# Warm-up matmuls between the first steps, exps spread over blocks, eight plain blocks first, three banks for eight blocks: one change to a linear-attention-and-MLP kernel

## The chip, the cores and the metric

The kernel runs on one core of one Trainium2 chip. The metric is the device time of one execution in microseconds (us). A profile of the same execution shows a span that is about 1.8 us shorter than that time. Each timed run also records the mean clock that TensorE was granted. For a comparison, the changed kernel and the kernel before ran in turn on the same chip; "ratio" below is the mean time of one kernel's fast runs over the mean of the other's in the same rounds, so it is not quite the ratio of the medians that are quoted.

## The reference, cut to what matters

```
# q, k, v: (8 batches, 8 heads, 576 positions, 64), float32
q_s = exp(q - max_d q);  q_s = q_s / sum_d q_s
k_s = exp(k - max_s k);  k_s = k_s / sum_s k_s
kv  = einsum('bhsd,bhse->bhde', k_s, v)
x   = einsum('bhsd,bhde->bhse', q_s, kv)       # then (4608, 512)
h   = x @ w_in                                  # (512, 2048)
g   = h * sigmoid(h)
out = g @ w_out                                 # (2048, 512)
```

## The kernel before

The work is cut into nine chunks of 512 rows; a batch has 576 rows. For chunk 0 the first product is done over the whole of batch 0 in 16 "wide" blocks of 576 columns. For the others it is done in 16 blocks `mm1` of 512 columns. After each block ScalarE computes a tanh into `sg` and VectorE multiplies it into `GT` (this is the silu), which frees the block's bank of the accumulator `PS`. The second product is plain for chunk 0 (16 blocks `mm2_plain`) and a seven-product scheme (`prod`) from chunk 1 on. That scheme needs differences of the weights (`t_op`: T1 to T4, once) and of the activations (`s_op`: S1 to S4, per chunk), all on VectorE. Between the blocks, a list of plans places the attention steps of the next batch: exps on ScalarE, sums on GpSimd or VectorE, normalisation of q, a transposition of q (by TensorE for batches 0 and 1, by a transposing DMA from batch 2 on), a key-value product on TensorE, and the input product `xt` of the next chunk.

The program hands each engine its instructions in the order in which they are written; a plan at unit `u` is written before block `u`.

```
def mm1(t, fb):
    bank = hb[0] % (2 if t == 1 else 3)        # chunk 1 has two banks, later chunks three
    hb[0] += 1
    mm1_mm(t, fb, bank, range(NC))
    mm1_silu(t, fb, bank)                      # ScalarE tanh, then VectorE product
...
def mm2_plain(t, fc):                          # uses banks 2 to 5
    for tb in range(4):
        nc.tensor.matmul(out=PS[:, 2 + tb, :], lhsT=GTS[t % 2][:, fc, ...], rhs=W2[:, fc, :], ...)
...
def heat(n, bank=5):                           # warm-up: the result is never read
    for _ in range(n):
        nc.tensor.matmul(out=PS[:, bank, :], lhsT=warm[:, 0:128], rhs=warm, start=True, stop=True)
...
heat(20)
... loads issued by GpSimd in this order: W1 (five parts), batch 1's q and k,
    W2[0:4], batch 1's v, W2[4:8]
...
# chunk 0's plain blocks and chunk 1's blocks a1 (b1 is the first of these units)
units += [lambda i=i: mm2_plain(0, i) for i in range(6)] + a1[:1]
for i in range(6, NFB):
    units += [a1[i - 5], lambda i=i: mm2_plain(0, i)]
units += a1[NFB - 5:]
...
plan(b1, lambda: (tr(1, 0, 0, 5, 6), tr(1, 0, 5, J, 7)))        # first transposition, batch 1
plan(b1 + 2, lambda: (tr(1, 1, 0, 5, 6), tr(1, 1, 5, J, 7)))    # second transposition
plan(b1 + 3, lambda: kv_both(1))
...
plan(b1 + 18, lambda: q_transpose(2))                           # the transposing DMA, batch 2
plan(b1 + 23, lambda: kv_both(2))
plan(b1 + 28, lambda: t_op(3, nc.vector, 0, 4))                 # T3
plan(b1 + 30, lambda: t_op(3, nc.vector, 4, 8))
for i, x in enumerate((28, 30)):
    plan(b1 + x, lambda i=i: xt(2, i))                          # needs the transposed q of batch 2
plan(begin[2], lambda: (mm2_plain_out(0), hb.__setitem__(0, 0)))  # evictions of banks 2 to 5
```

The softmax here doesn't subtract the row's maximum and nothing guards it: scores larger than these inputs give would overflow.

Of the kernel before, what the change touches and what calls it, by code (L numbers as in the profile page):

```python
# [17 lines left out]
def kernel(  # L18
# [72 lines left out]
    def load(b, name, src, cc, eng):  # L91
        t = ld.tile([128, 2, J * D], FP32, name=name)
        st[b][name, cc] = t
        x = src[b].rearrange("(g r) (p j) d -> g (r p) (j d)", r=2, j=J)
        eng.dma_start(out=t, in_=x.rearrange("g x y -> x g y")[:, 2 * cc:2 * cc + 2, :])  # L95
# [7 lines left out]
    def exp_q(b, cc):  # L103
        if "eq" not in st[b]:
            st[b]["eq"] = ap.tile([128, J, NG * D], BF16, name="eq", bufs=2)
        nc.scalar.activation(out=half(st[b]["eq"], cc), in_=jgd(b, "qt", cc), func=ACT.Exp)  # L106

    def exp_k(b, cc):
        nc.scalar.activation(out=half(ek, cc), in_=jgd(b, "kt", cc), func=ACT.Exp)  # L109

    def vcast(b, cc, eng, g0=0, g1=2):
        o = vaug[:, :, 2 * cc + g0:2 * cc + g1, 0:D]
        i = jgd(b, "vt", cc)[:, :, g0:g1, :]
        copy(eng, o, i)

    def qsum_pair(b, cc):
        e = half(st[b]["eq"], cc)
        t1 = ap.tile([128, J, 2, D // 2], FP32, name="t1")
        t2 = ap.tile([128, J, 2, D // 4], FP32, name="t2", bufs=2)
        nc.gpsimd.tensor_tensor(  # L120
            out=t1, in0=e[:, :, :, 0:D // 2], in1=e[:, :, :, D // 2:D], op=ALU.add
        )
        nc.gpsimd.tensor_tensor(
            out=t2, in0=t1[:, :, :, 0:D // 4], in1=t1[:, :, :, D // 4:D // 2], op=ALU.add
        )
        st[b]["t2", cc] = t2

    def qsum_end(b, cc):
        new_zq(b)
        nc.vector.reduce_sum(out=st[b]["zq"][:, cc], in_=st[b]["t2", cc], axis=AX.X)  # L130
        nc.vector.reciprocal(out=st[b]["rzq"][:, cc], in_=st[b]["zq"][:, cc])
# [16 lines left out]
    def qnorm(b, cc, eng):  # L148
        e = half(st[b]["eq"], cc)
        r = st[b]["rzq"][:, cc]  # L150
        eng.tensor_tensor(  # L151
            out=e, in0=e, in1=r[:, :, :, None].to_broadcast([128, J, 2, D]), op=ALU.mult
        )
# [12 lines left out]
    def tr(b, cc, j0, j1, bank):  # L166
        t = PS[:, bank, :].bitcast(BF16)
        for j in range(j0, j1):
            nc.tensor.transpose(  # L169
                out=t[:, (j - j0) * 128:(j - j0 + 1) * 128],  # L170
                in_=st[b]["eq"][:, j, cc * 128:(cc + 1) * 128],
                identity=ident,
            )

    def trcopy(b, cc, j0, j1, bank, eng=nc.vector):
        t = PS[:, bank, :].bitcast(BF16)[:, 0:(j1 - j0) * 128].rearrange("x (j y) -> x j y", y=128)
        copy(eng, new_qt(b)[:, j0:j1, cc, :], t)
# [13 lines left out]
    def kvcopy(b, c0=0, c1=2):  # L191
        kp = PS[:, 6:8, 0:256].rearrange("p r (c x) -> p r c x", x=128)[:, :, c0:c1, 0:E1]
        rz = ap.tile([128, 2, 2], FP32, name="rz", bufs=2)[:, :, 0:c1 - c0]
        nc.vector.reciprocal(out=rz, in_=kp[:, :, :, D])
        for c in range(c0, c1):
            nc.vector.tensor_tensor(
                out=kvn[b % 3][:, c],
                in0=kp[:, :, c - c0, 0:D],
                in1=rz[:, :, c - c0, None].to_broadcast([128, 2, D]),
                op=ALU.mult,  # L200
            )

    def kv_both(b):
        kv(b, 0)
        kv(b, 1)
        kvcopy(b)
# [11 lines left out]
    def xt_mm(b, cc, col, n, bank, dst):  # L218
        for r in range(2):
            for s in range(2):  # L220
                h = slice(s * 64, (s + 1) * 64)
                nc.tensor.matmul(  # L222
                    out=PS[r * 64:(r + 1) * 64, bank + s, dst:dst + n],
                    lhsT=kvn[b % 3][h, cc, r, :],
                    rhs=st[b]["qT"][h, col // P:(col + n) // P, cc, r * 64:(r + 1) * 64],
                )

    def xt_evac(t, cc, bank, d0, d1, o0, eng):
        o = XTS[t % 2][:, 2 * cc:2 * cc + 2, o0:o0 + d1 - d0]
        copy(eng, o, PS[:, bank:bank + 2, d0:d1])  # L230
# [33 lines left out]
            GTS[0][:, fb, :].rearrange("p (a n) -> p a n", a=2), S,  # L264
        )

    hb = [0]

    def mm1_mm(t, fb, bank, cs):
        o0 = pieces(t)[0][3]  # L270
# [11 lines left out]
        silu(t, fb, PS[:, bank, o0:TCH], GTS[t % 2][:, fb, o0:TCH], TCH - o0)  # L282

    def mm1(t, fb):
        bank = hb[0] % (2 if t == 1 else 3)
        hb[0] += 1
        mm1_mm(t, fb, bank, range(NC))
        mm1_silu(t, fb, bank)
# [10 lines left out]
    def mm2_plain(t, fc):  # L299
        for tb in range(4):  # L300
            nc.tensor.matmul(  # L301
                out=PS[:, 2 + tb, :],
                lhsT=GTS[t % 2][:, fc, tb * 128:(tb + 1) * 128],
                rhs=W2[:, fc, :],
                start=(fc == 0),
                stop=(fc == NFB - 1),
            )

    def mm2_plain_out(t):
        for ms in ((1, 2), (3, 0)):  # L310
            ow = mp.tile([128, 2, DM], FP32, name="ow", bufs=3)
            for i, m in enumerate(ms):
                if i == 0:
                    nc.scalar.activation(out=ow[:, i], in_=PS[:, 2 + m], func=ACT.Copy, scale=OS)
                else:
                    nc.vector.tensor_scalar_mul(out=ow[:, i], in0=PS[:, 2 + m], scalar1=OS)
                store(t, m * 128, ow[:, i])
# [116 lines left out]
    def heat(n, bank=5):  # L434
        for _ in range(n):
            nc.tensor.matmul(out=PS[:, bank, :], lhsT=warm[:, 0:128], rhs=warm, start=True, stop=True)
# [7 lines left out]
    def load_w2(f0, f1):  # L444
        nc.gpsimd.dma_start(
            out=W2[:, f0:f1, :],
            in_=w_out[f0 * 128:f1 * 128, :].rearrange("(fc p) o -> p fc o", p=128),
        )
# [34 lines left out]
    exp_k(0, 1)  # L483
    xt_mm(0, 0, 0, 320, 4, 0)
    xt_mm(0, 0, 320, 256, 0, 0)
    vcast(0, 1, nc.scalar, 0, 1)
    vcast(0, 1, nc.vector, 1, 2)
    trcopy(0, 1, 0, 5, 2, nc.scalar)
    trcopy(0, 1, 5, J, 3)
    kv(0, 1)  # L490
    kvcopy(0, 1, 2)
    xt_evac(0, 0, 4, 0, 320, 0, nc.scalar)
    xt_evac(0, 0, 0, 0, 256, 320, nc.vector)
    xt_mm(0, 1, 0, 320, 6, 0)
# [10 lines left out]
    def plan(u, f):  # L505
        at.setdefault(u, []).append(f)
# [26 lines left out]
    ORDER = (1, 5, 6, 2, 7, 4, 3)  # L533
    a1 = a_units(1)

    units += [lambda i=i: mm2_plain(0, i) for i in range(6)] + a1[:1]
    for i in range(6, NFB):
        units += [a1[i - 5], lambda i=i: mm2_plain(0, i)]
    units += a1[NFB - 5:]
    for t in range(2, NCH):  # L540
        begin[t] = len(units)
        bs = b_units(t - 1, ORDER)
# [76 lines left out]
            for cc in range(2):  # L619
                load(b, name, src, cc, eng)  # L620

    plan(8, lambda: (exp_q(1, 0), qsum_pair(1, 0)))
    plan(9, lambda: exp_q(1, 1))
    plan(11, lambda: (qsum_end(1, 0), qnorm(1, 0, nc.gpsimd), qsum_pair(1, 1)))
    plan(12, lambda: exp_k(1, 0))
    plan(13, lambda: load_w2(8, 12))
    plan(14, lambda: exp_k(1, 1))
    plan(b1, lambda: (tr(1, 0, 0, 5, 6), tr(1, 0, 5, J, 7)))
    plan(b1, lambda: (qsum_end(1, 1), qnorm(1, 1, nc.vector)))
    plan(b1, lambda: (trcopy(1, 0, 0, 5, 6, nc.scalar), trcopy(1, 0, 5, J, 7)))  # L630
    plan(b1, lambda: (vcast(1, 0, nc.scalar, 0, 1), vcast(1, 0, nc.vector, 1, 2)))
    plan(b1, lambda: (load_w2(12, 16), load(2, "qt", q, 0, nc.gpsimd)))
    plan(b1, lambda: nc.gpsimd.tensor_copy(GTS[1][:, :, 0:64], GTS[0][:, :, TCH:S]))
    plan(b1, lambda: (load(2, "qt", q, 1, nc.gpsimd), load(2, "kt", k, 0, nc.gpsimd)))
    plan(b1 + 2, lambda: (tr(1, 1, 0, 5, 6), tr(1, 1, 5, J, 7)))
    plan(b1 + 2, lambda: (trcopy(1, 1, 0, 5, 6, nc.scalar), trcopy(1, 1, 5, J, 7)))
    plan(b1 + 2, lambda: (vcast(1, 1, nc.scalar, 0, 1), vcast(1, 1, nc.vector, 1, 2)))
    plan(b1 + 2, lambda: load(2, "kt", k, 1, nc.gpsimd))
    plan(b1 + 3, lambda: kv_both(1))
    plan(b1 + 4, lambda: (load(2, "vt", v, 0, nc.gpsimd), load(2, "vt", v, 1, nc.gpsimd)))  # L640
    plan(b1 + 4, lambda: xt(1, 0))
    plan(b1 + 5, lambda: xt(1, 1))

    plan(b1 + 9, lambda: t_op(1, nc.vector, 0, 4))
    plan(b1 + 11, lambda: t_op(1, nc.vector, 4, 8))
    for i, x in enumerate((12, 14)):
        plan(b1 + x, lambda i=i: exp_q(2, i))
        plan(b1 + x + 1, lambda i=i: qsum(2, i, 0))
# [2 lines left out]
    plan(b1 + 18, lambda: q_transpose(2))  # L651
    for i, x in enumerate((19, 21)):
        plan(b1 + x, lambda i=i: vcast(2, i, nc.scalar))
    plan(b1 + 23, lambda: t_op(2, nc.vector, 0, 4))
    plan(b1 + 24, lambda: t_op(2, nc.vector, 4, 8))
    plan(b1 + 25, lambda: t_op(4, nc.vector, 0, 4))
    plan(b1 + 26, lambda: t_op(4, nc.vector, 4, 8))
    plan(b1 + 28, lambda: t_op(3, nc.vector, 0, 4))
    plan(b1 + 30, lambda: t_op(3, nc.vector, 4, 8))
    plan(b1 + 23, lambda: kv_both(2))  # L660
    plan(b1 + 22, lambda: loads(3, nc.sync))
    for i, x in enumerate((28, 30)):
        plan(b1 + x, lambda i=i: xt(2, i))
    plan(begin[2], lambda: (mm2_plain_out(0), hb.__setitem__(0, 0)))

    for t in range(2, NCH - 1):
        b = t + 1
# [58 lines left out]
```

## Time and profile before

| | before |
|---|---|
| time, median of 3 runs | 277.97 us (277.51 to 278.47) |
| span of the profiled execution | 276.2 us |
| TensorE busy | 262.9 us (95%) |
| mean granted clock in that execution | 0.991 |
| first `prod` of chunk 1's output (the start of chunk 2's stretch) | 69.40 us |

The first fence is from the page of the kernel before: busy time, share and instruction count of each engine, then the granted TensorE clock in tenths, in 40 equal slices of the span.

```profile
PE 262.9 (95%) x2339; PEld 168.7 (61%) x2367; DVE 199.3 (72%) x292; ACT 159.7 (58%) x239; POOL 67.4 (24%) x60
...
PEclk9979999999999999999999999999999999999998
```

TensorE is nearly full, and slice 3 (a 7 among nines) shows a short fall of its clock. The view by stretches of the kernel before tells which: columns are the stretch, its length, then busy us (and instructions) of TensorE, weight loads, VectorE, ScalarE and GpSimd, then the granted clock, the DMA share and GB/s.

```profile
11.70:15.11 3.41, 2.03 (x61) 1.31 (x61) 2.59 (x8) 2.84 (x4) 3.41 (x6) 1.00 1.16 181
15.11:18.53 3.42, 3.17 (x18) 1.98 (x15) 0.86 (x2) 0.72 (x2) 1.00 (x2) 0.50 1.19 211
```

The clock is half from 15.11 to 18.53 us, just after a stretch of the same length in which TensorE was busy 2.03 of 3.41 us. The waits of TensorE in the kernel before follow, for 8 to 34 us (the first four of five lines) and for 34 to 69.3 us (who waited, for whom, us in total, how often, the longest).

```profile
PE PS L169 <- DVE eq L151: 1.2, 1, 1.2
PE PS L183 <- ACT vaug L87: 0.9, 2, 0.7
PE PS L252 <- DVE GT L245: 0.6, 2, 0.5
PE PS L222 <- ACT XT L87: 0.6, 1, 0.6
```

```profile
PE PS L169 <- DVE eq L151: 1.6, 1, 1.6
PE PS L272 <- DVE GT L245: 0.7, 2, 0.5
PE PS L301 <- DVE GT L245: 0.2, 1, 0.2
```

Line 252 is a wide block and line 272 a block of later chunks, each waiting until VectorE's silu product frees a bank; line 169 is a transposition that waits for the normalised q. Lines 183 and 222 are batch 0's key-value and input products, which wait 0.7 and 0.6 us for ScalarE at the places where the change puts its warm-up matmuls. The 1.6 us is batch 1's second transposition. From 69.4 to 90 us TensorE has no wait that the view lists. The timeline of the kernel before (start, us, engine, line, what, and in brackets the idle time before it): First TensorE at the end of chunk 1, where line 222 is the input product `xt` and line 362 the first `prod`; then VectorE in chunk 2, where line 245 is a silu product and line 336 an S difference.

```profile
61.84 0.92 PE L272 MATMUL PS<-XT,W 128*128 128x448 bf16 x4
62.70 0.57 PE L222 MATMUL PS<-qT,kvn 64*64 64x128 bf16 x8
...
65.47 1.70 PE L272 MATMUL PS<-XT,W 128*128 128x448 bf16 x8 [0.16 <-DVE GT L245]
67.68 1.89 PE L272 MATMUL PS<-XT,W 128*128 128x512 bf16 x7 [0.50 <-DVE GT L245]
69.40 0.71 PE L362 MATMUL PS<-W,GT 128*128 128x256 f16 x5
```

```profile
77.43 1.22 DVE L245 SCALAR_TENSOR_TENSOR GT<-sg,PS 128x512 f16<-128x512 f32 x2
78.57 2.29 DVE L336 TENSOR_TENSOR S<-GT 128x2048 f16<-128x2048 f16 x1
80.78 1.27 DVE L245 SCALAR_TENSOR_TENSOR GT<-sg,PS 128x512 f16<-128x512 f32 x2
```

### The profile page before, as it was taken

What the parts mean: (1) busy time and instruction counts of PE and PEld (TensorE: products, weight loads), DVE (VectorE), ACT (ScalarE), POOL (GpSimd) and SP (SyncE); (2) the same over time, 40 slices, a digit from 0 to 9 for tenths busy, and PEclk for the clock granted to TensorE, in tenths of its full rate; (3) what the DMA queues carried; (4) which work ended last, traced back from release to release, by engine and by line L of the source; (5) the groups of instructions that cost most, each with busy time, mean ns of one, the idle gap of its engine ahead of it and who ended that gap; (6) DMA issues with size and microseconds to landing.
All of it is one profiled execution on the core that took longest, in us unless ns stands there. A gap on an engine that the chain in (4) does not pass through costs nothing.

```text
span 276.2 us, 5761 instructions
## 1 busy us (share of the span) xinstructions
PE 262.9 (95%) x2339; PEld 168.7 (61%) x2367; DVE 199.3 (72%) x292; ACT 159.7 (58%) x239; POOL 67.4 (24%) x60
## 2 busy tenths in 40 slices
PE   8689979998999999999999999999999999999993
PEld 3357634453666566656665666566656665666782
DVE  2946783868998489848984898489937674767643
ACT  5757934868764676457645774577464446444410
POOL 1743691320090009000900090009100000000003
PEclk9979999999999999999999999999999999999998
DMA  7999989669998376937692869251224003300444
GB/s 263 321 201 368 297 129 338 237 80 392 297 298 287 79 190 195 291 80 197 183 298 61 207 186 296 47 114 37 50 60 95 0 2 76 78 0 0 94 99 114
DMA packets 35498, 45.85 MB, mean 166 GB/s; under 512 B 16208, under 2 KB 20048, under 8 KB 35472
## 3 DMA queue, kind: packets, MB, share of 16 engines
q1 hardware_dynamic: 29568, 33.69, 43.9%
q0 software_dynamic: 5584, 11.54, 16.3%
q8 instruction: 18, 0.29, 0.4%
q10 hardware_dynamic: 320, 0.26, 0.3%
q14 instruction: 8, 0.07, 0.1%
HBM read 36.70 MB, written 9.44 MB: 167 GB/s over the span
## 4 chain that ended last, share of the span: by engine, by line
PE 87%; DMA 3%; DVE 3%; ACT 2%; issue 2%; SPq 1%; ACTq 0%
PE PS L272 38%; PE PS L362 36%; PE PS L301 4%; PE PS L252 4%; DMA vt<-in_v_dram 3%; PE PS L183 2%; PE PS L222 2%; DVE GT L245 1%; ACT sg L244 1%; SPq L95 1%; DVE eq L151 1%; ACT eq L106 1%; ACT XT L87 0%; PE PS L169 0%; ACT vaug L87 0%
## 5 line engine op out<-in xcount | busy, mean ns | idle before, releaser
L245 DVE SCALAR_TENSOR_TENSOR GT<-sg,PS 128x512 f16<-128x512 f32 (+2 forms) x144 | 96.7, 680 | 57.7 <-ACT sg L244 57.3
L244 ACT ACTIVATE sg<-PS 128x512 f32<-128x512 f32 (+2 forms) x144 | 85.6, 597 | 83.3 <-PE PS L272 75.5
L272 PE MATMUL PS<-XT,W 128*128 128x512 bf16 (+1 forms) x484 | 124.3, 375 | 2.0 <-DVE GT L245 0.7
L272 PEld LDWEIGHTS <-W 128*128 128x128 bf16 x512 | 49.9, 98 | 39.3 <-issue 1.3
L362 PEld LDWEIGHTS <-S 128*128 128x128 f16 x512 | 49.2, 98 | 16.6 <-issue 1.2
L151 POOL TENSOR_TENSOR eq<-eq,rzq 128x1152 bf16<-128x1152 bf16 x13 | 27.4, 2116 | 112.4 <-ACT sg L244 99.8
L362 PEld LDWEIGHTS <-GT 128*128 128x128 f16 x384 | 37.1, 98 | 13.1 <-issue 1.2
L362 PE MATMUL PS<-W,S 128*128 128x256 f16 x256 | 33.0, 273 | 0.1
L362 PE MATMUL PS<-W,GT 128*128 128x256 f16 x256 | 32.7, 273 | 0.1
L362 PE MATMUL PS<-T,S 128*128 128x256 f16 x256 | 32.7, 273 | 0.0
L336 DVE TENSOR_TENSOR S<-GT 128x2048 f16<-128x2048 f16 (+1 forms) x17 | 25.0, 1471 | 0.0
L584 POOL DMA_DIRECT2D out_dram<-ow x4 | 2.2, 550 | 75.7 <-DVE ow L569 75.7
L106 ACT ACTIVATE eq<-qt 128x1152 bf16<-128x1152 f32 x16 | 18.6, 1162 | 2.5 <-DMA qt<-in_q_dram 2.5
L109 ACT ACTIVATE ek<-kt 128x1152 bf16<-128x1152 f32 x16 | 18.6, 1165 | 1.3 <-DMA kt<-in_k_dram 1.3
L87 ACT CAST XT<-PS 128x1024 bf16<-128x1024 f32 (+2 forms) x18 | 17.3, 961 | 2.9 <-PE PS L222 2.9
L142 DVE TENSOR_REDUCE zq<-eq 128x18 f32<-128x1152 bf16 x12 | 16.1, 1344 | 3.9 <-ACT eq L106 3.9
L252 PE MATMUL PS<-XT,W 128*128 128x288 bf16 x128 | 17.8, 302 | 0.9 <-DVE GT L245 0.6
L301 PE MATMUL PS<-W,GT 128*128 128x512 f16 x64 | 16.4, 379 | 0.2 <-DVE GT L245 0.2
L252 PEld LDWEIGHTS <-W 128*128 128x128 bf16 x128 | 13.1, 103 | 5.6 <-issue 1.7
L362 PE MATMUL PS<-T,GT 128*128 128x256 f16 x128 | 16.5, 273 | 0.0
L89 POOL CAST vaug<-vt 128x1152 bf16<-128x1152 f32 x10 | 16.3, 1654 | 0.0
L336 DVE TENSOR_TENSOR S<-GT,S 128x2048 f16<-128x2048 f16 x8 | 14.0, 1750 | 0.0
(58 smaller groups left out, 154.5 us busy)
## 6 DMA issues: line engine op xcount, KB each, us to landing
out_dram<-ow SPq DMA_DIRECT2D x64, 128.0 KB, 2.4
qt<-in_q_dram SPq DMA_DIRECT2D x12, 576.0 KB, 4.6
kt<-in_k_dram SPq DMA_DIRECT2D x12, 576.0 KB, 6.5
vt<-in_v_dram SPq DMA_DIRECT2D x12, 576.0 KB, 7.4
qt<-in_q_dram POOLq DMA_DIRECT2D x4, 576.0 KB, 11.6
kt<-in_k_dram POOLq DMA_DIRECT2D x4, 576.0 KB, 12.9
vt<-in_v_dram POOLq DMA_DIRECT2D x4, 576.0 KB, 13.5
W<-in_moe_w_out_dram POOLq DMA_DIRECT2D x4, 512.0 KB, 11.9
```

The source lines that it names most:

```text
L87: eng.copy(out=o, in_=i)
L89: eng.tensor_copy(o, i)
L106: nc.scalar.activation(out=half(st[b]["eq"], cc), in_=jgd(b, "qt", cc), func=ACT.Exp)
L109: nc.scalar.activation(out=half(ek, cc), in_=jgd(b, "kt", cc), func=ACT.Exp)
L151: eng.tensor_tensor(out=e, in0=e, in1=r[:, :, :, None].to_broadcast([128, J, 2, D]), op=ALU.mult)
L244: nc.scalar.activation(out=s, in_=i, func=ACT.Tanh, scale=OS)
L245: nc.vector.scalar_tensor_tensor(out=o, in0=s, scalar=1.0, in1=i, op0=ALU.add, op1=ALU.mult)
L252: nc.tensor.matmul(out=PS[:, 2 * (fb % 3) + n, 0:S // 2], lhsT=W1[:, c, fb * 128:(fb + 1) * 128], rhs=XTS[0][:, c, n * (S // 2):(n + 1) * ...
L272: nc.tensor.matmul(out=PS[:, bank, o0:TCH], lhsT=W1[:, c, fb * 128:(fb + 1) * 128], rhs=XTS[t % 2][:, c, o0:TCH], start=(c == 0), stop=(c ...
L301: nc.tensor.matmul(out=PS[:, 2 + tb, :], lhsT=GTS[t % 2][:, fc, tb * 128:(tb + 1) * 128], rhs=W2[:, fc, :], start=(fc == 0), stop=(fc == N ...
L336: nc.vector.tensor_tensor(out=SS[i - 1][:, f], in0=in0[:, f], in1=in1[:, f], op=op)
L362: nc.tensor.matmul(out=PS[:, bank, m * HN:(m + 1) * HN], lhsT=a[:, fc, m * 128:(m + 1) * 128], rhs=bb[:, fc, :], start=(first and fc == 0) ...
```

## The change

Its intent is to fill TensorE's small waits at the start: keep its clock up between batch 0's steps, give ScalarE's exps room, hide batch 1's preparation behind eight plain blocks, and give chunk 1's last blocks a third bank. The diff, cut to its core:

```diff
-    hb = [0]
+    hb = [0, 2]                      # next block, and now also the number of banks
...
-        bank = hb[0] % (2 if t == 1 else 3)
+        bank = hb[0] % hb[1]
...
+    heat(3, 6)                       # after the first input product of batch 0
     vcast(0, 1, nc.scalar, 0, 1)
...
     kvcopy(0, 1, 2)
+    heat(2, 3)
...
-    units += [lambda i=i: mm2_plain(0, i) for i in range(6)] + a1[:1]
-    for i in range(6, NFB):
-        units += [a1[i - 5], lambda i=i: mm2_plain(0, i)]
-    units += a1[NFB - 5:]
+    units += [lambda i=i: mm2_plain(0, i) for i in range(8)]
+    for i in range(8, NFB):
+        units += [a1[i - 8], lambda i=i: mm2_plain(0, i)]
+    units += a1[NFB - 8:]
...
-    plan(8, lambda: (exp_q(1, 0), qsum_pair(1, 0)))
-    plan(9, lambda: exp_q(1, 1))
-    plan(11, lambda: (qsum_end(1, 0), qnorm(1, 0, nc.gpsimd), qsum_pair(1, 1)))
-    plan(12, lambda: exp_k(1, 0))
-    plan(14, lambda: exp_k(1, 1))
+    plan(9, lambda: (exp_q(1, 0), qsum_pair(1, 0)))
+    plan(11, lambda: exp_q(1, 1))
+    plan(12, lambda: (qsum_end(1, 0), qnorm(1, 0, nc.gpsimd), qsum_pair(1, 1)))
+    plan(13, lambda: exp_k(1, 0))
+    plan(15, lambda: (exp_k(1, 1), load_w2(8, 12)))
...
-    plan(b1 + 2, lambda: (tr(1, 1, 0, 5, 6), tr(1, 1, 5, J, 7)))
-    plan(b1 + 3, lambda: kv_both(1))
+    plan(b1 + 4, lambda: (tr(1, 1, 0, 5, 6), tr(1, 1, 5, J, 7)))
+    plan(b1 + 5, lambda: kv_both(1))
...                                   # T1, T2, T4 three to thirteen units earlier
-    plan(b1 + 28, lambda: t_op(3, nc.vector, 0, 4))
-    plan(b1 + 30, lambda: t_op(3, nc.vector, 4, 8))
-    for i, x in enumerate((28, 30)):
+    plan(b1 + 24, lambda: (mm2_plain_out(0), hb.__setitem__(0, 2), hb.__setitem__(1, 3)))
+    for i, x in enumerate((26, 29)):
         plan(b1 + x, lambda i=i: xt(2, i))
-    plan(begin[2], lambda: (mm2_plain_out(0), hb.__setitem__(0, 0)))
+    plan(begin[2] + 5, lambda: t_op(3, nc.vector, 0, 4))
+    plan(begin[2] + 8, lambda: t_op(3, nc.vector, 4, 8))
```

More of the change, by code (lines that the diff above doesn't have):

```diff
@@ L309, in mm2_plain_out @@
     def mm2_plain_out(t):
-        for ms in ((1, 2), (3, 0)):
+        for ms in ((0, 1), (2, 3)):
             ow = mp.tile([128, 2, DM], FP32, name="ow", bufs=3)
@@ L620, in loads @@
                 load(b, name, src, cc, eng)
-    plan(8, lambda: (exp_q(1, 0), qsum_pair(1, 0)))
-    plan(9, lambda: exp_q(1, 1))
-    plan(11, lambda: (qsum_end(1, 0), qnorm(1, 0, nc.gpsimd), qsum_pair(1, 1)))
-    plan(12, lambda: exp_k(1, 0))
-    plan(13, lambda: load_w2(8, 12))
-    plan(14, lambda: exp_k(1, 1))
+    plan(9, lambda: (exp_q(1, 0), qsum_pair(1, 0)))
[3 more added lines that the diff above has]
+    plan(15, lambda: (exp_k(1, 1), load_w2(8, 12)))
     plan(b1, lambda: (tr(1, 0, 0, 5, 6), tr(1, 0, 5, J, 7)))
+    plan(b1, lambda: (trcopy(1, 0, 0, 5, 6, nc.scalar), trcopy(1, 0, 5, J, 7)))
     plan(b1, lambda: (qsum_end(1, 1), qnorm(1, 1, nc.vector)))
-    plan(b1, lambda: (trcopy(1, 0, 0, 5, 6, nc.scalar), trcopy(1, 0, 5, J, 7)))
     plan(b1, lambda: (vcast(1, 0, nc.scalar, 0, 1), vcast(1, 0, nc.vector, 1, 2)))
@@ L634 @@
     plan(b1, lambda: (load(2, "qt", q, 1, nc.gpsimd), load(2, "kt", k, 0, nc.gpsimd)))
-    plan(b1 + 2, lambda: (tr(1, 1, 0, 5, 6), tr(1, 1, 5, J, 7)))
-    plan(b1 + 2, lambda: (trcopy(1, 1, 0, 5, 6, nc.scalar), trcopy(1, 1, 5, J, 7)))
-    plan(b1 + 2, lambda: (vcast(1, 1, nc.scalar, 0, 1), vcast(1, 1, nc.vector, 1, 2)))
-    plan(b1 + 2, lambda: load(2, "kt", k, 1, nc.gpsimd))
-    plan(b1 + 3, lambda: kv_both(1))
-    plan(b1 + 4, lambda: (load(2, "vt", v, 0, nc.gpsimd), load(2, "vt", v, 1, nc.gpsimd)))
-    plan(b1 + 4, lambda: xt(1, 0))
-    plan(b1 + 5, lambda: xt(1, 1))
-    plan(b1 + 9, lambda: t_op(1, nc.vector, 0, 4))
-    plan(b1 + 11, lambda: t_op(1, nc.vector, 4, 8))
+    plan(b1 + 2, lambda: vcast(1, 1, nc.scalar))
+    plan(b1 + 4, lambda: (tr(1, 1, 0, 5, 6), tr(1, 1, 5, J, 7)))
+    plan(b1 + 4, lambda: (trcopy(1, 1, 0, 5, 6, nc.scalar), trcopy(1, 1, 5, J, 7)))
+    plan(b1 + 4, lambda: load(2, "kt", k, 1, nc.gpsimd))
+    plan(b1 + 5, lambda: kv_both(1))
+    plan(b1 + 5, lambda: (load(2, "vt", v, 0, nc.gpsimd), load(2, "vt", v, 1, nc.gpsimd)))
+    plan(b1 + 6, lambda: xt(1, 0))
+    plan(b1 + 7, lambda: xt(1, 1))
+    plan(b1 + 6, lambda: t_op(1, nc.vector, 0, 4))
+    plan(b1 + 7, lambda: t_op(1, nc.vector, 4, 8))
+    plan(b1 + 10, lambda: t_op(2, nc.vector, 0, 4))
+    plan(b1 + 11, lambda: t_op(2, nc.vector, 4, 8))
     for i, x in enumerate((12, 14)):
@@ L653 @@
         plan(b1 + x, lambda i=i: vcast(2, i, nc.scalar))
-    plan(b1 + 23, lambda: t_op(2, nc.vector, 0, 4))
-    plan(b1 + 24, lambda: t_op(2, nc.vector, 4, 8))
-    plan(b1 + 25, lambda: t_op(4, nc.vector, 0, 4))
-    plan(b1 + 26, lambda: t_op(4, nc.vector, 4, 8))
-    plan(b1 + 28, lambda: t_op(3, nc.vector, 0, 4))
-    plan(b1 + 30, lambda: t_op(3, nc.vector, 4, 8))
+    plan(b1 + 20, lambda: t_op(4, nc.vector, 0, 4))
+    plan(b1 + 22, lambda: t_op(4, nc.vector, 4, 8))
     plan(b1 + 23, lambda: kv_both(2))
     plan(b1 + 22, lambda: loads(3, nc.sync))
-    for i, x in enumerate((28, 30)):
+    plan(b1 + 24, lambda: (mm2_plain_out(0), hb.__setitem__(0, 2), hb.__setitem__(1, 3)))
+    for i, x in enumerate((26, 29)):
         plan(b1 + x, lambda i=i: xt(2, i))
-    plan(begin[2], lambda: (mm2_plain_out(0), hb.__setitem__(0, 0)))
+    plan(begin[2] + 5, lambda: t_op(3, nc.vector, 0, 4))
+    plan(begin[2] + 8, lambda: t_op(3, nc.vector, 4, 8))
     for t in range(2, NCH - 1):
```

## The prediction

> **What bounds the kernel now.** On the page, TensorE is busy 262.9 of 276.2 us (95%), and the chain of waits is 87% TensorE. The timeline shows a dense stream from 44 us to the end, and the change leaves that work as it is. What can be won lies before 69 us:
>
> 1. Clock. The stretch view shows the granted clock at 0.50 from 15.1 to 18.5 us, after a stretch (11.7 to 15.1) where TensorE was busy 2.03 of 3.41 us. The Trainium skill ("TensorE: Matmul & The Clock Gate", Part 1) says a free-running monitor window of about 3.4 us with too little matmul activity halves the clock; the trace agrees in length. Some 3.1 us of wide matmuls (128x288, 0.123 us each warm) ran at half speed: 1.5 us lost.
> 2. Wide blocks wait 0.18 and 0.45 us (28 to 30 us) for VectorE's silu products, because two exps of 1.16 us stand close together on ScalarE, which has 0.33 us spare per 0.98 us block.
> 3. Chunk 0's plain blocks wait 0.23 us behind block 14's silu, then 1.65 us at the second transposition for VectorE's normalisation of q (1.74 us).
> 4. Chunk 1's last blocks wait 0.16 and 0.50 us with two banks.
>
> **What the change does.**
> - Five warm-up matmuls (0.22 us each) fall into waits of 0.72 and 0.60 us: the window's busy share rises from 60% to about 90%. I expect the clock to stay full: -1.5 us, 80% sure. The first-layer weights still arrive about 0.4 us before use.
> - Four exps over seven blocks are 4.6 us of ScalarE against 2.3 us spare: each costs 0.2 to 0.4 us, and the first sum on VectorE (0.45 + 0.27 us) also delays a block. I estimate 0.9 us of waits where there were 0.6: +0.3. The last exp now follows block 14's silu: -0.2.
> - Batch 1's first normalised q (GpSimd, 2.12 us) is made a block later while TensorE comes sooner: the first transposition, which did not wait, now waits about 0.4 us.
> - The second transposition comes after four plain blocks (0.86 us each) instead of two: 1.65 us of wait shrinks to about 0.5. The second-layer weights' second part (landing near 37.5 us) arrives about when block 4 wants it. -1.1 us.
> - Batch 2's loads do not come sooner by as much as the stream: up to 0.5 us at batch 2's key-value product.
> - Three banks for eight consecutive blocks of 0.77 us: ScalarE has 8 x 0.54 + 2 x 1.01 + 2 x 0.54 = 7.4 us against 7.2 us of TensorE, and the first block uses bank 2, which must first be evicted (0.4 us). Waits stay near the old 0.7 us.
> - T3's differences (1.37 us) move into chunk 2 on VectorE, the evictions (1.28 us) out: even.
>
> Sum: -1.5 +0.1 +0.4 -1.1 +0.2 = about -2 us, all on the critical path, since the stream after 69 us only shifts.
>
> **Predicted:** 275.9 us, 8 in 10 between 274.5 and 277.4. Faster by over 2%: 0.03; within 2%: 0.96; slower by over 2%: 0.01.
>
> **What would show it.** Right: clock 1.0 from 15 to 19 us; a wait for q's normalisation of 0.2 to 0.8 us at the second transposition and a new one of 0.2 to 0.6 at the first; chunk 2 starting about 2 us earlier. Wrong: the clock still drops; waits of over 1 us for weights or batch 2's loads; or the last eight blocks wait well over 1 us, or hardly at all.

## The result, and the profile after

| | before | changed |
|---|---|---|
| time, first set, median of 4 each | 277.76 us | 278.36 us (278.28 to 278.57) |
| ratio, 95% interval | | 1.0019 (0.9998 to 1.0039) |
| second set, median of 11 and 6 | 277.87 us | 277.93 us |
| ratio, 95% interval | | 1.0003 (0.9988 to 1.0017) |
| span of the first profiled execution | 276.2 us | 276.8 us |
| first `prod` in it | 69.40 us | 68.84 us |

The time is the same. The predicted gain of 2 us is not there, and 278.36 us lies above the predicted range. The page of the changed kernel, the same two lines:

```profile
PE 263.0 (95%) x2343; PEld 167.9 (61%) x2372; DVE 200.1 (72%) x291; ACT 160.5 (58%) x239; POOL 68.0 (25%) x60
...
PEclk9999999999999999999999999999999999999999
```

The stretches of the changed kernel that answer to those of before:

```profile
11.70:15.11 3.41, 3.05 (x65) 1.55 (x66) 2.65 (x9) 2.90 (x4) 3.41 (x6) 1.00 1.10 161
15.11:18.53 3.42, 3.17 (x30) 2.37 (x25) 1.48 (x3) 1.89 (x3) 1.12 (x2) 1.00 1.20 207
```

The clock did stay full: TensorE was busy 3.05 of 3.41 us, and the next stretch held 30 matmuls instead of 18. TensorE's waits in the changed kernel, for 8 to 34 (the first four of six lines), 34 to 69.3 and 69.4 to 90 us:

```profile
PE PS L169 <- DVE eq L151: 1.6, 2, 1.5
PE PS L169 <- POOL eq L151: 0.5, 1, 0.5
PE PS L252 <- DVE GT L245: 0.4, 1, 0.4
PE PS L252 <- DMA W<-in_moe_w_in_dram: 0.3, 1, 0.3
```

```profile
PE PS L222 <- DMA qT<-eq: 1.4, 1, 1.4
PE PS L169 <- DVE eq L151: 0.7, 1, 0.7
```

```profile
PE PS L272 <- DVE GT L245: 0.8, 2, 0.7
```

Besides the clock, two things are as foretold: the second transposition waits 0.7 us instead of 1.6, and the first now waits 0.5. Chunk 1's last blocks are no longer listed, which the prediction had named as a sign that it was wrong ("or hardly at all"). Three waits are new and were not foretold: 1.4 us for the transposing DMA of batch 2's q, 0.8 us in chunk 2, and 0.3 us for the first-layer weights. The timeline of the changed kernel at the end of chunk 1 (TensorE), and in chunk 2 (VectorE; the second line is one half of T3):

```profile
60.08 0.25 PE L222 MATMUL PS<-qT,kvn 64*64 64x128 bf16 x4
61.75 0.36 PE L222 MATMUL PS<-qT,kvn 64*64 64x384 bf16 x4 [1.42 <-DMA qT<-eq]
62.04 2.44 PE L272 MATMUL PS<-XT,W 128*128 128x448 bf16 x12
...
68.84 1.04 PE L362 MATMUL PS<-W,GT 128*128 128x256 f16 x8
```

```profile
77.42 0.63 DVE L245 SCALAR_TENSOR_TENSOR GT<-sg,PS 128x512 f16<-128x512 f32 x1
77.96 2.35 DVE L346 TENSOR_TENSOR W<-W 128x1024 f16<-128x1024 f16 x1
80.24 0.67 DVE L245 SCALAR_TENSOR_TENSOR GT<-sg,PS 128x512 f16<-128x512 f32 x1
```

The first four matmuls of `xt(2, 0)` use batch 1's q and run at once; the next four want batch 2's and wait. The chain of waits of the changed kernel, in order of time (start, us, what), says what they wait for:

```profile
53.84 2.12 POOL eq L151
55.96 0.02 issue
55.97 5.74 DMA qT<-eq
61.71 0.04 issue
61.75 0.36 PE PS L222 x4
```

GpSimd's normalisation ends at 55.96, the transposing DMA is issued, and 5.74 us later it has landed. In the kernel before the same DMA was issued at 57.27 us and landed at 62.86 us; its `xt(2, 0)` began at 62.70 us and needed that data four matmuls later. There it fitted with next to no slack: the first of those matmuls started at 62.91 us. The change brought `xt(2, 0)` forward by 2.6 us (62.70 to 60.08) but the DMA by 1.3 us only.

In chunk 2, one silu product that stood directly after another one (77.43 us, x2, in the kernel before) now stands behind half of T3, which took 2.35 us, and the TensorE block that needs its bank starts late.

### The profile page after: what moved, and what is told of

The parts are those of the page before. It is cut to its first block, busy times and chain, and to the rows that moved or that the text cites. A ratio compares the mean times of both kernels' runs of the same rounds, so it can differ in the third digit from the quotient of the medians.

```text
span 276.8 us, 5771 instructions
## 1 busy us (share of the span) xinstructions
PE 263.0 (95%) x2343; PEld 167.9 (61%) x2372; DVE 200.1 (72%) x291; ACT 160.5 (58%) x239; POOL 68.0 (25%) x60
## 4 chain that ended last, share of the span: by engine, by line
PE 74%; DMA 7%; DVE 6%; POOL 5%; issue 5%; ACT 3%; POOLq 0%; ACTq 0%
PE PS L272 34%; PE PS L362 34%; DMA qt<-in_q_dram 5%; DMA qT<-eq 2%; PE PS L222 2%; PE PS L301 2%; PE PS L183 2%; POOL eq L151 2%; DVE S L336 1%; POOL W L439 1%; ACT eq L106 1%; DVE GT L245 1%; DVE W L346 1%; ACT sg L244 1%; DVE zq L142 1%
## 5 line engine op out<-in xcount | busy, mean ns | idle before, releaser
L272 PEld LDWEIGHTS <-W 128*128 128x128 bf16 x512 | 49.9, 98 | 40.2 <-issue 2.5
L336 DVE TENSOR_TENSOR S<-GT 128x2048 f16<-128x2048 f16 (+1 forms) x17 | 24.3, 1427 | 0.0
L252 PE MATMUL PS<-XT,W 128*128 128x288 bf16 x128 | 16.8, 286 | 1.2 <-DVE GT L245 0.4
L252 PEld LDWEIGHTS <-W 128*128 128x128 bf16 x128 | 12.3, 97 | 5.6 <-issue 2.0
L336 DVE TENSOR_TENSOR S<-GT,S 128x2048 f16<-128x2048 f16 x8 | 13.1, 1642 | 0.0
```

The lines of the kernel that those rows point to most:

```text
L252: nc.tensor.matmul(out=PS[:, 2 * (fb % 3) + n, 0:S // 2], lhsT=W1[:, c, fb * 128:(fb + 1) * 128], rhs=XTS[0][:, c, n * (S // 2):(n + 1) * ...
L272: nc.tensor.matmul(out=PS[:, bank, o0:TCH], lhsT=W1[:, c, fb * 128:(fb + 1) * 128], rhs=XTS[t % 2][:, c, o0:TCH], start=(c == 0), stop=(c ...
L336: nc.vector.tensor_tensor(out=SS[i - 1][:, f], in0=in0[:, f], in1=in1[:, f], op=op)
```

## The experiments

My theory after reading the two profiles (A): the front did gain, and two moves that I had counted as harmless took it back, `xt(2)` (1.4 us) and T3 (about 1 us). The rival (B): chunk 2 is paced by VectorE, GpSimd or the loads, so an earlier start is only waited away there. A third question was how much of the clock's 1.5 us is real. Every kernel below gave a correct result. The kernel before was run beside them in the same rounds; its median was 277.66 to 277.88 us. The runs were made on four chips, so variants are compared by their ratios to the kernel before of their own rounds. For the changed kernel I take the ratio 1.0003 of its larger set; with the first set's 1.0019 every gain over it below would be 0.4 us larger.

**Without the warm-up matmuls.**

```diff
-    heat(3, 6)
...
-    heat(2, 3)
```

> The changed kernel without its five new warm-up matmuls. Theory A (the warm-up keeps the clock full, but about half of its 1.5 us is given back because the wide blocks then catch up with the first-layer weights): the granted clock falls to 0.5 for about 3.4 us near 15 us, the waits for the weights (0.35 to 0.5 us) go, and the kernel is 0.5 to 1.0 us slower than the changed kernel, ratio to the kernel before 1.003 to 1.006. Rival B (weights and exps pace the wide phase alone, so the clock there is worth nothing): within 0.2 us of the changed kernel. It also shows where the first-layer weights land without the warm-up: if their landing goes back from 24.6 to about 23.4 us, the warm-up itself delays them; if it stays or scatters, it is run-to-run.

Measured: 278.27 us median (277.79 to 279.00), ratio to before 1.0012 (0.9991 to 1.0034). The profile shows the clock at 0.50 for 3.41 us from 14.86 us on. But the six timed runs fall apart: two have a mean granted clock of 0.991 and 0.994 and take 278.74 and 279.00 us; the other four have 0.997 to 1.000 and take 277.79 to 278.60 us. A fall of the clock for 3.41 us at half speed lowers the mean over 276 us by 0.006, so only the first two had it. Neither theory was right as put: the fall costs something near 0.8 us here (means of two and of four runs), but it happens in some executions only. The last part of the first-layer weights landed at 24.1 us, between the 23.4 us of the first profile before and the 24.6 us of the first profile after; over all fourteen profiles it lands between 23.4 and 24.6 us with and without the warm-up (24.6 us also in the second profile of the kernel before, which has none), so the warm-up does not delay it, and the 0.3 us wait for it is a matter of the run (the second profile of the changed kernel does not have it).

**T3 back before chunk 2.**

```diff
-    plan(begin[2] + 5, lambda: t_op(3, nc.vector, 0, 4))
-    plan(begin[2] + 8, lambda: t_op(3, nc.vector, 4, 8))
+    plan(b1 + 28, lambda: t_op(3, nc.vector, 0, 4))
+    plan(b1 + 30, lambda: t_op(3, nc.vector, 4, 8))
```

> The changed kernel with T3's two differences back among chunk 1's last blocks, as in the kernel before. Theory A (in chunk 2 they stand in front of silu products on VectorE and one runs at 2.35 us instead of 0.69 beside GpSimd's normalisation; that costs TensorE about 1 us): the waits of 0.66 and 0.19 us in chunk 2 vanish, 0.7 to 1.2 us faster than the changed kernel, ratio to before 0.998. Rival B (chunk 2's pace is set by batch 3's loads and GpSimd, so what is saved is waited for elsewhere): within 0.3 us of the changed kernel. Rival C: the cost comes back as waits among chunk 1's last blocks.

Measured: 276.86 us median, ratio 0.9966 (0.9947 to 0.9985), about 1 us better than the changed kernel's 1.0003. In 56 to 90 us the profile lists one wait of TensorE, the transposing DMA; chunk 2's waits are gone and none came back among chunk 1's last blocks. A holds, B and C do not.

**The input products of chunk 2 back to units 28 and 30.**

```diff
-    for i, x in enumerate((26, 29)):
+    for i, x in enumerate((28, 30)):
```

> The changed kernel with chunk 2's input products (which wait 1.42 us for the transposing DMA of q) back at units 28 and 30. Theory A: that wait falls below 0.2 us, because blocks of chunk 1 run meanwhile; 1.0 to 1.4 us faster than the changed kernel, ratio to before 0.997. Rival B (VectorE's and GpSimd's chain in chunk 2 paces TensorE, and starting earlier only makes the waits there longer): chunk 2 starts 1.2 us earlier but waits there grow, gain under 0.5 us.

Measured: 276.54 us median, ratio 0.9950 (0.9933 to 0.9967), 1.5 us better than 1.0003. TensorE's timeline in this kernel:

```profile
58.27 3.19 PE L272 MATMUL PS<-XT,W 128*128 128x448 bf16 x16
61.39 0.51 PE L222 MATMUL PS<-qT,kvn 64*64 64x128 bf16 x8
...
67.05 1.04 PE L362 MATMUL PS<-W,GT 128*128 128x256 f16 x8
```

Four blocks now run while the DMA is under way, `xt(2, 0)` does not wait, and the first `prod` starts at 67.05 us. The waits of 0.8 us in chunk 2 did not grow. A holds.

**Both.**

> Both undone at once (T3 early, input products late). Theory A: the two savings add up, 1.8 to 2.5 us faster than the changed kernel, about 276.2 us, ratio to before 0.993 to 0.995: the gain that was predicted for the front. Rival B: no more than the better of the two alone.

Measured: 275.22 us median, ratio 0.9904 (0.9882 to 0.9925), 2.7 us better than 1.0003; the sum of the two alone is 1.0 + 1.5 us. The first listed wait of TensorE after the second transposition is gone: 56 to 90 us has none. The savings add up, so chunk 2 has no pace of its own that swallows them.

**The kernel before, profiled once more.**

> The kernel before, profiled once more. Theory A: the fall of the clock near 15 us in its first profile is an accident[...], as the granted clocks of the timed runs suggest (0.990 and 0.992 in 2 of 11 runs, 0.997 to 1.000 in the others); this profile will most likely show a full clock, the first-layer weights waited for by 0.2 to 0.8 us, and chunk 2 starting about 0.5 to 0.8 us earlier than in the first profile (69.4 us). Rival B: the clock falls in every execution, and the mean granted clock of a run does not tell it.

Measured: one run of 278.47 us, granted clock 0.99: the clock fell again. The timed runs decide the question. In the four sets of 11 runs of the kernel before, 13 of 44 have a mean granted clock under 0.995; they take 278.20 us on average, the other 31 take 277.70 us. So the fall happened in three executions of ten and cost about 0.5 us. Rival B fails: the mean does tell it, since the three profiled executions with a fall have a mean of 0.990 to 0.994 and the eleven without one 0.996 or more. Over all kernels that have the five warm-up matmuls, 1 of 64 timed runs lies under 0.995, so the warm-up does prevent the fall; what was wrong is its worth.

**Both halves of T3 at unit 5 of chunk 2.**

```diff
-    plan(begin[2] + 8, lambda: t_op(3, nc.vector, 4, 8))
+    plan(begin[2] + 5, lambda: t_op(3, nc.vector, 4, 8))
```

> The changed kernel with both halves of T3 at unit 5 of chunk 2, so the second runs before GpSimd's normalisation starts. Theory A (the cost is the slowing of VectorE beside GpSimd, 2.35 us instead of 0.69): the second half takes 0.7 us and two thirds or more of the wait in chunk 2 goes, 0.5 to 1.0 us faster than the changed kernel. Rival B (the cost is VectorE work standing in front of silu products, whatever its speed, since the S differences beside GpSimd then slow down instead): the waits stay within 0.3 us of the changed kernel's 0.85.

Measured: 276.69 us median, ratio 0.9965 (0.9943 to 0.9987), the same as with T3 out of chunk 2 altogether. Its only listed wait from 56 to 90 us is 1.2 us for the transposing DMA. VectorE's timeline in this kernel:

```profile
71.98 1.29 DVE L346 TENSOR_TENSOR W<-W 128x1024 f16<-128x1024 f16 x2
...
76.85 1.22 DVE L245 SCALAR_TENSOR_TENSOR GT<-sg,PS 128x512 f16<-128x512 f32 x2
77.99 2.29 DVE L336 TENSOR_TENSOR S<-GT 128x2048 f16<-128x2048 f16 x1
```

Both halves take 1.29 us together when GpSimd is idle. The slow instruction is now S3 (2.29 us, as in the kernel before), and it stands after the two silu products, not between them. So it was not the amount of VectorE's work that cost: T3, S3 and S4 together take 5.8 us in the changed kernel and 5.7 us here. It was which instruction got held up, and what stood behind it.

The holding up has a clear end. In the changed kernel GpSimd's two normalisations run from 75.57 for 4.19 us, to 79.76 us, the second of them from 77.65 us; the T3 half started at 77.96 us, after it, and ended 0.55 us after it. The Trainium skill ("SBUF — State Buffer", section "Who interferes with whom") says that a VectorE instruction with two inputs in SBUF contends with a GpSimd instruction that reads SBUF, and that whichever comes first holds the shared ports for its whole instruction. The trace agrees: 2.35 us beside GpSimd, 0.64 us each without it. Not everything on VectorE is slower there: the silu product at 77.42 us, which reads one of its inputs from the accumulator, took 0.63 us beside the same normalisations.

**The exps back in their old blocks** (in the kernel with T3 early and `xt` late).

```diff
-    plan(9, lambda: (exp_q(1, 0), qsum_pair(1, 0)))
-    plan(11, lambda: exp_q(1, 1))
...
+    plan(8, lambda: (exp_q(1, 0), qsum_pair(1, 0)))
+    plan(9, lambda: exp_q(1, 1))
...
```

> The kernel with T3 early and the input products late (275.2 us), with batch 1's exps back in their old blocks (8, 9, 12, 14). Theory A (four exps of 1.16 us do not fit ScalarE's spare time however they are spread, and the first normalised q comes later with them): the same time within 0.4 us, with two larger waits in place of three smaller ones. Rival B (the spreading brought the intended gain): 0.5 us or more slower.

Measured: 275.05 us median, ratio 0.9899 (0.9876 to 0.9921), against 275.22 us and 0.9904 with the exps spread. Spreading them is worth nothing that can be measured. With the old places ScalarE waits 1.1 us for batch 1's q to land and TensorE for ScalarE, but the first transposition then does not wait; with the new places it is the other way round.

**Two banks for all of chunk 1** (in the kernel with T3 early and `xt` late).

```diff
-    plan(b1 + 24, lambda: (mm2_plain_out(0), hb.__setitem__(0, 2), hb.__setitem__(1, 3)))
+    plan(begin[2], lambda: (mm2_plain_out(0), hb.__setitem__(0, 0), hb.__setitem__(1, 3)))
```

> The kernel with T3 early and the input products late (275.2 us), with two banks for all of chunk 1 and the evictions at the start of chunk 2, as before. Theory A (eight consecutive blocks need the third bank: the chain from a block's end through ScalarE and VectorE is about 1.6 us against 0.77 us of the one block between): 2 to 4 us slower. Rival B (as I predicted: no gain from the third bank): within 0.5 us.

Measured: 276.61 us median, ratio 0.9958 (0.9937 to 0.9978), 1.4 us slower than with three banks (275.22 us). It is less than the 2 to 4 us that I expected, but clear. The edit also moves the evictions back to the start of chunk 2, but the profile lists no wait there. TensorE's waits from 56 to 70 us in this kernel are the line below; with three banks there are none.

```profile
PE PS L272 <- DVE GT L245: 1.4, 4, 0.5
```

**The changed kernel again.**

> The changed kernel itself, timed beside the others of this call and profiled again. It should repeat 1.002 of the kernel before; its profile should again show a full clock near 15 us, the wait for the transposing DMA of about 1.4 us and the waits of about 0.85 us in chunk 2. Where the first-layer weights' last part lands (24.6 us in its first profile, 23.6 to 24.4 in six profiles of others with the same loads) should vary.

Measured: 277.93 us median, ratio 1.0003; clock full in all six runs (0.996 to 1.000). The profile repeats the waits: 1.1 us for the transposing DMA, 0.7 for the second and 0.4 for the first transposition, 0.8 in chunk 2. The first-layer weights' last part landed at 23.4 us this time.

**Only the warm-up matmuls, in the kernel before.**

```diff
     xt_mm(0, 0, 320, 256, 0, 0)
+    heat(3, 6)
...
     kvcopy(0, 1, 2)
+    heat(2, 3)
```

> The kernel before with only the five warm-up matmuls. My prediction's term of 1.5 us (the clock falls in every execution): 1.0 to 1.5 us faster than the kernel before. Theory A (it falls in about a quarter of the executions, 5 of 22 timed ones, and costs about 0.7 us there): 0.0 to 0.4 us faster on average, no run below a granted clock of 0.995, and a narrower spread of times.

Measured: 277.40 us median against 277.87 us of the kernel before; five runs lie between 277.33 and 277.48 us, and one at 280.81 us with a granted clock of 0.994, which I did not expect and cannot explain. With that run the ratio is 1.0008 (0.9969 to 1.0047), so on average nothing is shown; by the medians the warm-up is worth about 0.5 us, which is more than falls in 5 of the 11 runs beside it (0.5 us each) would explain; six runs do not settle that. A gain of 1.0 to 1.5 us is not there. Its profile has a full clock, and ScalarE's timeline shows where the faster clock goes (line 244 is a tanh, line 106 an exp of batch 1's q):

```profile
23.70 0.65 ACT L244 ACTIVATE sg<-PS 128x576 f32<-128x576 f32 x1 [0.33 <-PE PS L252]
25.07 1.16 ACT L106 ACTIVATE eq<-qt 128x1152 bf16<-128x1152 f32 x1 [0.72 <-DMA qt<-in_q_dram]
26.14 0.63 ACT L244 ACTIVATE sg<-PS 128x576 f32<-128x576 f32 x1
```

The wide blocks now come sooner than batch 1's q, so ScalarE stands 0.72 us before the exp, the next tanh is late, and TensorE waits 1.00 us for its bank (0.18 us in the first profile before). The first transposition starts at 33.12 us, 0.56 and 1.02 us sooner than in the two profiles with the fallen clock (33.68 and 34.14 us), not 1.5.

**An attempt at a better one: the second-layer weights ahead of v.**

```diff
     load_w2(0, 4)
+    load_w2(4, 8)
     load(1, "vt", v, 0, nc.gpsimd)
     load(1, "vt", v, 1, nc.gpsimd)
-    load_w2(4, 8)
...                       # and: T3 early, xt late, nine plain blocks first, batch 1's
...                       # second transposition and its followers one unit later
```

> An attempt at a better one: T3 early, input products late (275.2 us), the second-layer weights' second part loaded ahead of batch 1's v, nine plain blocks first, batch 1's second transposition and what follows one unit later, and bank 1 first after the evictions. Theory A (the front is held by the loads: plain block 4 wants weights that land at 38 us, and the second transposition waits about 1 us for VectorE): that wait falls below 0.3 us and the kernel takes 274.2 to 274.7 us, 0.5 to 1.0 us faster than the best so far. Rival B (v now lands too late for batch 1's key-value product): a new wait there of 0.5 us or more and no gain.

Measured: 275.35 us median, ratio 0.9913 (0.9896 to 0.9930), no better than 275.22 us. The wait at the second transposition is gone from the list, and another came in its place; the listed wait of TensorE from 52 to 90 us, and VectorE's timeline just before it:

```profile
PE PS L272 <- DVE GT L245: 1.2, 1, 1.2
```

```profile
56.26 0.68 DVE L346 TENSOR_TENSOR T<-W,T 128x1024 f16<-128x1024 f16 x1
56.86 0.17 DVE L194 RECIPROCAL rz<-PS 128x4 f32<-128x4 f32 x1
57.07 0.49 DVE L196 TENSOR_TENSOR kvn<-PS,rz 128x128 bf16<-128x128 f32 x2
57.48 1.28 DVE L316 TENSOR_SCALAR ow<-PS 128x512 f32<-128x512 f32 x2
58.67 1.67 DVE L245 SCALAR_TENSOR_TENSOR GT<-sg,PS 128x448 f16<-128x448 f32 x3
```

Neither A nor B as put: TensorE did not wait for v (ScalarE did, 2.7 us in two waits, against 1.0 us in the kernel of 275.22 us), but the block order now lets half of T4, the key-value copies and two evictions stand in front of three silu products.

**The same with VectorE's work thinned there.**

```diff
-    plan(b1 + 22, lambda: t_op(4, nc.vector, 4, 8))
-    plan(b1 + 23, lambda: kv_both(2))
+    plan(b1 + 27, lambda: t_op(4, nc.vector, 4, 8))
+    plan(b1 + 24, lambda: kv_both(2))
...                       # and both halves of T3 at unit 5 of chunk 2
```

> The last attempt (275.35 us) with VectorE's work around the evictions thinned: T3's halves both at unit 5 of chunk 2 (where they cost nothing in an earlier run), T4's second half five units later, batch 2's key-value product one unit later. Theory A (the transposition's wait that was removed came back as one wait of 1.2 us at block 10 of chunk 1, because VectorE does two evictions, a T4 half and the key-value copies before the silu products that free the bank): that wait falls below 0.4 us, 274.2 to 274.8 us. Rival B (VectorE is full over the whole stretch, so the wait moves to a later block): within 0.3 us of 275.35.

Measured: 274.83 us median (274.46 to 275.50), ratio 0.9895 (0.9879 to 0.9912). The wait fell from 1.2 to 0.2 us, and chunk 2 has none. This is the fastest by the median, 2.9 us under the kernel before of its rounds (277.75 us), but its interval overlaps those of the kernel with both moves undone (0.9904) and with the old exps (0.9899), so that it beats those two is not shown.

## Why the prediction was wrong

The range was missed by 1 us (278.36 against at most 277.4; the second set, 277.93, misses it by 0.5), and the forecast of a gain failed. Point by point:

1. **"I expect the clock to stay full: -1.5 us, 80% sure" is mis-sized.** The clock does stay full. But I took one profile for the rule. In 44 timed runs of the kernel before, the clock fell in 13, and those took 0.5 us longer, so on average the fall costs about 0.15 us (0.5 x 13/44). Why a fall costs so much less than 1.5 us, the kernel before with the warm-up shows: with a full clock ScalarE waits 0.72 us for batch 1's q, and TensorE's first transposition comes only 0.56 to 1.02 us sooner than in the two profiles with a fall.
2. **The exps, "+0.3"**: the exps in the old places gave the same time within 0.2 us, so this small term is within what could be measured.
3. **The first transposition's new wait of 0.4 us** and **the second's 0.5 instead of 1.65** were right: 0.45 and 0.68 us in the first profile.
4. **"Batch 2's loads do not come sooner by as much as the stream: up to 0.5 us at batch 2's key-value product" named the wrong place and missed the term.** No such wait is listed. What does not come sooner is the transposed q of batch 2, behind GpSimd's normalisation and a DMA of 5.7 us. The change asks for it two units earlier, and the old place had no slack. This wait is 1.1 to 1.4 us, and undoing the move gained 1.5 us. I had read the moved `xt` as part of the bank question and never asked when its input lands.
5. **"Three banks ...: waits stay near the old 0.7 us" was too low a gain.** The waits went to none; without the third bank the kernel is 1.4 us slower. I had added up ScalarE's work (7.4 against 7.2 us) and charged 0.4 us for the eviction, where the profile shows no wait for it.
6. **"T3's differences (1.37 us) move into chunk 2 on VectorE, the evictions (1.28 us) out: even" failed as a step.** The sums are indeed nearly even, but one half of T3 fell beside GpSimd's normalisation, took 2.35 us instead of 0.64, and stood in front of a silu product that TensorE was about to need. It cost about 1 us; the same work three units earlier costs nothing. With it fails the step "all on the critical path, since the stream after 69 us only shifts": from the first `prod` to chunk 2's key-value product the stream took 15.73 us before and 16.90 us in the changed kernel, in the two profiles of the ledger below.

Two profiles with a full clock give the ledger: the kernel before with the warm-up, and the changed kernel's second. The first transposition starts at 33.12 and 32.75 us (0.37 gained, with its new wait), the first `prod` at 68.77 and 67.72 (1.05 gained, although 1.1 us of it was lost to the transposing DMA), and chunk 2's key-value product at 84.50 and 84.62 (all given back to T3). So the front's gain exists, and with the two moves undone it shows in the time: 275.2 us. That these 2.7 us come near the forecast 2 is in part luck: the clock's term was too large by about 1.3 us, the third bank's too small by 0.7 us (the old waits) to 1.4 us (the two-bank run).

What stays open is the single run of 280.81 us, what decides in which executions the clock falls, and whether the second attempt really beats the kernel with only the two moves undone.

## What to carry to other kernels

A stage that starts earlier asks for each of its inputs earlier: for every step that a change moves, look up when its data lands and how much slack it had, before adding up busy times. A sum of durations does not tell the cost of a moved instruction; ask what stands behind it on its engine, and what shares its ports at that moment. And take a clock state from many runs, not from the one that was profiled.

## What the Trainium skill lacked or had wrong

- "TensorE: Matmul & The Clock Gate" (section "Why this matters for your kernels") advises against TensorE idle gaps of over about 3 us. Here the clock fell in three profiles whose longest wait of TensorE in the 3.41 us before was 0.60, 0.72 and 0.94 us; TensorE was busy 1.94, 2.03 and 1.87 us of these 3.41, and with 3.05 us in the changed kernel the clock stayed full. So that advice alone does not foresee this fall; where between these shares the limit lies was not measured. The window's length (Part 1) agrees: the fall lasted 3.41 us in each of three profiles that show it.
- The same page (Part 1) says of the first matmuls that the warm-up varies from run to run because the window runs freely. It does not say that a later fall can differ from run to run as well: 13 of 44 runs of one kernel had it.
- "DMA: Bandwidth & Descriptors" (section "Latency and other measured facts") gives an effective 261 GB/s for transposing DMAs. Here one of 128x2304 in 2-byte elements (590 KB) took 5.7 us from issue to landing, which is 103 GB/s (2.8 us of it is the issuing instruction on SyncE), and the median of the six in this execution is 4.6 us; neither that section nor the one on the DMA transpose has a latency for one of this size.
- "SBUF — State Buffer" (section "Who interferes with whom") was right, and its size here is: a two-input VectorE instruction of 0.64 us took 2.35 us beside GpSimd's normalisation and ended 0.55 us after it.
